# Half-chunks of two heads side by side in a triangular solve: 36 products per chunk in place of 72, and Q before K in one line

## The chip, the cores and the metric

One NeuronCore of one Trainium2 chip runs the whole program. The metric is the device time of one execution in microseconds; several executions are timed and their median is quoted.

## The reference

A delta-rule attention (4 batches, 8 heads, 768 tokens, head size 48) feeds two wide layers (384 to 2048 and back), one after the other.

```python
for t in range(S):
    y[:, :, t] = einsum('bhd,bhde->bhe', q[:, :, t], state)
    v_old = einsum('bhde,bhd->bhe', state, k_n[:, :, t])
    state = state + beta_t * einsum('bhd,bhe->bhde', k_n[:, :, t], v[:, :, t] - v_old)
x = y.transpose(0, 2, 1, 3).reshape(B * S, H * D)
h = x @ w_in;  x = softplus(h) @ w_out          # first layer
h = x @ w2_in; out = (h * cos(h)) @ w2_out      # second layer
```

`k_n` is `k` divided by its norm, per head and token.

## The kernel before

**Tiles.** The 768 tokens go in 24 chunks of C = 32. The 128 rows of a tile are the 4 batches times the 32 tokens of a chunk, and the 8 heads stand beside each other in the columns (8 x 48 = 384). A product for one head is a 128x128 stationary operand with four 32x32 (or 32-row) blocks on its diagonal, one per batch, against 48 moving columns. Every operand is kept as a pair of f16, a high and a low part, so a product is three passes, high by high, low by high and high by low (`HI_FIRST`): 3 x 8 = 24 PE products for all heads.

**Block diagonals.** The stationary tiles (`bdK`, `bdQ`, `bdA`, `bd2`, `bdG`, `bdT`) are zeroed once; then each chunk's rows are written into the diagonal blocks by DMAs in pieces of 64 f16. K and Q rows go from the buffer `kq` to DRAM (`kqd`) and back into `bdKQ`; keys, the masked scores and the coupling G go from `kp` through `kpd` into `bd2` and `bdG` (`load_2`); T goes through `tgd` into `bdT`, and for some odd chunks into a second tile that lies in `raw` (`bdU`).

**The solve.** Within a chunk, u has to solve a unit lower triangular 32x32 system per head and batch. It is cut into two halves of 16 tokens. `take_A` takes both diagonal 16x16 blocks of the Gram matrix (`abuf`) and the block that couples the halves (`kg`, later `bdG`). `solve` inverts the diagonal blocks for four chunks at once on VectorE, giving T. `step` then applies T to b, G to the result, adds that to b, and applies T again: the groups T, G, T, 24 products each, 72 in all. In all three the 16 upper tokens of a head and its 16 lower tokens share one 32x32 block. `take_b` and `take_u` split b and u into high and low parts between the groups: a ScalarE or VectorE copy for the high part, a VectorE subtraction for the low part.

**A chunk's serial path** (`step`, line 727): K rows by state into `psC0` (40 products), `bt` = that less v, `take_b`, T into `psC1`, `take_u`, G into `psC0`, `bt` plus that, `take_b`, T into `psC1`, `take_u`, the state update into `psC0` and `psC1` (48 products), the new state and its f16 parts, and on to the next chunk. The outputs y (Q rows by state, then scores by u) collect in `psY`. Two chunks fill a block of 256 tokens, which `moe_block(0, j)` sends through the first layer (`psH`, `accA`, `accB`). When all are done, the second layer runs six blocks of 512 tokens.

**Rows of a chunk.** `prep_k` transposes K on VectorE into `kq`: lines 554 to 557 write the main part and a tail of 8C columns. `prep_q` scales Q into the other row of the same buffer, and line 569 sends the first 32C columns of both rows to `kqd`. The buffer of chunk n is `kq[n % 4]`, [128, 2, 40C].

**Order.** Nothing is issued where it is written: `put` records operations with their keys, and a planner (`Plan`, lines 60 to 269) lists them per engine by estimated costs, with a priority from the backward pass. Where an operation may run on ScalarE or VectorE (`copy`), the planner also chooses the engine. The tile framework then adds the waits between the instructions that it finds to touch the same memory. Engines run their lists in order. All DMAs stand in SyncE's list.

Of the kernel before, what the change touches and what calls it, by code (L numbers as in the profile page):

```python
# [10 lines left out]
F32 = mybir.dt.float32  # L11
# [9 lines left out]
P = 128  # L21
# [267 lines left out]
def delta_moe_moe_kernel(ctx, tc, q, k, v, beta, mask, ident, w1, w2, out):  # L289
# [15 lines left out]
    mask_sb = const.tile([P, C + 4], F32, name="mask_sb")  # L305
# [19 lines left out]
    bdK, bdQ = bdKQ[:, 0], bdKQ[:, 1]  # L325
    bdA2 = att.tile([P, 44, B, X2], F16, name="bdA2")
# [8 lines left out]
    bt = att.tile([P, H, D], F32, name="bt")  # L335
    b16 = att.tile([P, 2, H, D], F16, name="b16")
# [6 lines left out]
    kpf = [pre.tile([P, 64 * C], F16, name=f"kp{i}") for i in range(4)]  # L343
    kpb = [x[:, 0:48 * C].rearrange("p (s h d l) -> p s h d l", s=3, h=H, l=2) for x in kpf]
    kgb = [x[:, 48 * C:].rearrange("p (h t l) -> p h t l", h=H, l=2) for x in kpf]
    kab = [pre.tile([P, H // 2, C, 2], F16, name=f"ka{i}") for i in range(2)]
    kqb = [pre.tile([P, 2, Z], F16, name=f"kq{i}") for i in range(4)]
# [27 lines left out]
    kpd = dr.tile([NS, P, C * 64], F16, name="kpd")  # L375
# [183 lines left out]
    def prep_q(n):  # L559
# [4 lines left out]
        qv = kq[:, 1, 0:32 * C].rearrange("p (s h t l) -> p s h t l", s=2, t=C, l=2)  # L564
# [3 lines left out]
        if n >= 4:  # L568
            dma(kqd[n].rearrange("p (s z) -> p s z", s=2), kq[:, :, 0:32 * C], [("kqd", n)],
                [("kq", s, i) for i in range(3)] + [("pre",)], 1.46, issue=0.8, slack=1.5, **A)  # L570
        elif n:
            dma(kqd[n, :, 0:32 * C], k_main(n), [("kqd", n, 0)], k_keys(n)[:1], 0.73, **A)
            dma(kqd[n, :, 32 * C:], kq[:, 1, 0:32 * C], [("kqd", n, 1)], [("kq", s, 1), ("kq", s, 2), ("pre",)], 0.73, **A)
# [67 lines left out]

    def take_P(n, ps, pk):
# [3 lines left out]
        tt(pm, ps, mask_sb[:, 0:C].unsqueeze(1).to_broadcast([P, H, C]), ALU.mult, [("sq",)],  # L646
# [5 lines left out]
            + [("kp", s, i) for i in (*range(2, 6), "z")] + [("pre",)], 1.46, slack=1.5, **A)  # L652

    def solve(g):
# [3 lines left out]
        put([("DVE", 0.602)], [("m",)], [("abuf", i) for i in range(4)] + PR, lambda e: nc.vector.transpose(  # L658
# [68 lines left out]
    def step(n):  # L727
# [337 lines left out]
```

## Time and profile before

| | us |
|---|---|
| median of 3 runs | 1021.29 (1019.23 to 1028.05) |
| the profiled execution | 1025.06 |
| its span, first to last instruction | 1023.3 |
| TensorE (PE) busy | 957.5 |
| VectorE (DVE) busy | 661.5 |
| ScalarE (ACT) busy | 675.1 |
| GpSimd (POOL) busy | 348.6 |

Busy times are sums over one execution. A row of the timeline gives start, duration, engine, line, operation, output<-inputs, and in brackets the time that its engine sat idle before it and what ended that. PEld is PE's loading of stationary operands, which runs beside its products. SPq is SyncE's queue, which issues the DMAs. [...]

### The profile page before, as it was taken

How to read it: one execution, taken by the hardware profiler on the slowest of the kernel's cores; microseconds unless marked ns; L12 is line 12 of the kernel's file. 1: busy time of each engine (PE TensorE's matmuls, PEld its weight loads, DVE VectorE, ACT ScalarE, POOL GpSimd, SP SyncE). 2: the span in 40 equal slices, each digit the busy share in tenths (PEclk: the TensorE clock that was granted, in tenths of full speed). 3: DMA queues.
4: the chain of work that ended last, by engine and by line, in shares of the span. 5: the costliest groups of instructions: out<-in, count | busy, mean ns of one | idle time of the engine just before them, and what ended most of it. 6: DMA issues, size and time to landing. Idle time of an engine off the chain costs nothing.

```text
span 1023.3 us, 27706 instructions
## 1 busy us (share of the span) xinstructions
PE 957.5 (94%) x11624; PEld 690.2 (67%) x11624; DVE 661.5 (65%) x1193; ACT 675.1 (66%) x1278; POOL 348.6 (34%) x323
## 2 busy tenths in 40 slices
PE   1777987999999999999999999999999999999998
PEld 1446976989889898999998888644444444444443
DVE  8899974568548755964766665785555555455554
ACT  5375766677868877786768778866555555455554
POOL 4012135224423632362233334553332323323232
PEclk9788998999999999999999999999999999999999
DMA  6988896785777678577678942111001010000000
GB/s 201 304 242 201 172 255 137 166 213 123 179 163 163 134 179 180 110 149 158 134 179 209 211 99 78 47 62 62 1 10 53 1 62 1 32 31 1 31 1 31
DMA packets 317164, 121.91 MB, mean 119 GB/s; under 512 B 281456, under 2 KB 297072, under 8 KB 317040
## 3 DMA queue, kind: packets, MB, share of 16 engines
q1 hardware_dynamic: 317040, 120.15, 48.6%
q8 instruction: 91, 1.49, 0.6%
q14 instruction: 33, 0.27, 0.1%
HBM read 73.45 MB, written 37.22 MB: 108 GB/s over the span
## 4 chain that ended last, share of the span: by engine, by line
PE 59%; DVE 10%; ACT 8%; SPq 8%; DMA 8%; issue 4%; POOL 2%; DVEq 0%; ACTq 0%; POOLq 0%
PE psH L827 15%; PE accA L889 12%; PE accB L889 9%; SPq L384 7%; PE psC L827 7%; PE psA L889 6%; PE psC L710 4%; PE psY L827 4%; PE psY L710 2%; DMA qt<-q_dram 1%; DMA kt<-k_dram 1%; DMA w<-w_dram 1%; PE psA L622 1%; ACT e L416 1%; DVE g L405 1%
## 5 line engine op out<-in xcount | busy, mean ns | idle before, releaser
L405 POOL TENSOR_TENSOR g<-g,g 128x512 f16<-128x512 f32 x189 | 227.3, 1203 | 508.9 <-ACT g L393 507.6
L827 PE MATMUL psH<-xt,w 128*128 128x256 f16 x1728 | 224.3, 273 | 0.0
L393 ACT ACTIVATE g<-g 128x512 f16<-128x512 f32 x191 | 120.1, 629 | 115.6 <-DVE g L409 69.2
L889 PEld LDWEIGHTS <-w 128*128 128x128 f16 x1728 | 160.7, 98 | 21.7 <-issue 2.8
L827 PEld LDWEIGHTS <-w 128*128 128x128 f16 x1728 | 158.3, 97 | 17.6 <-issue 0.2
L889 PE MATMUL accA<-g,w 128*128 128x256 f16 x1152 | 156.3, 274 | 2.3 <-POOL g L405 2.3
L889 PEld LDWEIGHTS <-v 128*128 128x128 f16 x864 | 84.5, 98 | 102.4 <-issue 0.5
L827 PEld LDWEIGHTS <-v 128*128 128x128 f16 x864 | 84.5, 98 | 100.4
L414 ACT ACTIVATE e<-e 128x512 f32<-128x512 f32 x96 | 60.4, 629 | 82.0 <-DVE e L409 81.9
L405 DVE TENSOR_TENSOR g<-psH,e 128x512 f32<-128x512 f32 x96 | 66.1, 688 | 59.4 <-ACT e L416 50.4
L889 PE MATMUL accB<-g,w 128*128 128x256 f16 x576 | 93.3, 273 | 0.0
L710 PEld LDWEIGHTS <-bdA 128*128 128x128 f16 x2256 | 74.5, 98 | 17.9 <-issue 14.6
L827 PE MATMUL psH<-xu,v 128*128 128x512 f16 x351 | 83.4, 379 | 0.0
L827 PE MATMUL psC<-xu,v 128*128 128x512 f16 x342 | 82.1, 379 | 0.0
L889 PE MATMUL accA<-g,v 128*128 128x512 f16 x288 | 78.0, 379 | 0.3 <-POOL g L405 0.3
L889 PE MATMUL accB<-g,v 128*128 128x512 f16 x288 | 77.8, 379 | 0.0
L889 PE MATMUL psA<-g,v 128*128 128x512 f16 x288 | 77.7, 379 | 0.0
L844 ACT ACTIVATE e<-psH 128x512 f32<-128x512 f32 x96 | 56.5, 588 | 29.9 <-PE psH L827 29.7
L416 ACT ACTIVATE e<-e,hpi 128x512 f32<-128x512 f32 x96 | 69.1, 721 | 2.9
L710 PE MATMUL psC<-u,bdA 128*128 128x48 f16 x1680 | 59.9, 185 | 9.7 <-DMA bdA<-kpd 4.1
L710 PEld LDWEIGHTS <-bdKQ 128*128 128x128 f16 x1840 | 58.7, 97 | 5.6 <-issue 3.5
L416 ACT ACTIVATE e<-e 128x512 f32<-128x512 f32 x96 | 59.9, 624 | 1.2
(151 smaller groups left out, 1479.5 us busy)
## 6 DMA issues: line engine op xcount, KB each, us to landing
kpd<-kp SPq DMA_DIRECT2D x24, 512.0 KB, 4.6
bdA<-kpd SPq DMA_DIRECT2D x96, 128.0 KB, 4.1
bdKQ<-kqd SPq DMA_DIRECT2D x92, 128.0 KB, 4.0
kqd<-kq SPq DMA_DIRECT2D x20, 512.0 KB, 4.7
raw<-w_dram SPq DMA_DIRECT2D x12, 768.0 KB, 5.0
w<-w_dram SPq DMA_DIRECT2D x10, 768.0 KB, 7.1
v<-w_dram SPq DMA_DIRECT2D x10, 768.0 KB, 6.0
qt<-q_dram SPq DMA_DIRECT2D x24, 256.0 KB, 4.5
```

The source lines that it names most:

```text
L384: put([("SP", issue)], w, r, lambda e: nc.sync.dma_start(out=dst, in_=src), dma=eng_us, **kw)
L393: nc.scalar.activation(out=out, in_=in_, func=AF.Copy, scale=scale)
L405: put(var, w, r, lambda e: eng[e].tensor_tensor(out=out, in0=a, in1=b, op=op), port=True, **kw)
L414: nc.scalar.activation(out=out, in_=in_, func=func, scale=scale)
L416: nc.scalar.activation(out=out, in_=in_, func=func, scale=scale, bias=bias)
L622: nc.tensor.matmul(ps[:, h], lhsT=w, rhs=x, start=(i == 0), stop=(i == len(ops) - 1))
L710: nc.tensor.matmul(ps[:, h, 0:D], lhsT=lhs(h), rhs=mov[:, h], start=(first and i == 0 and h == 0), stop=(last and i == len(passes) - 1 and ...
L827: nc.tensor.matmul(hp[:, i] if ph == 0 else hp, lhsT=w[:, l, kc * P:(kc + 1) * P], rhs=xv[:, m * KC + kc], start=(kc == 0 and idx == 0), s ...
L844: nc.scalar.activation(out=ev, in_=hv, func=AF.Abs, scale=sc)
L889: nc.tensor.matmul(acc[c], lhsT=w[:, l, c * P:(c + 1) * P], rhs=rhs, start=(f == 0 and idx == 0 and (ph == 1 or c != 1)), stop=(f == NF - ...
```

## The change

Two heads, h and h + 4, now share a 32-row block in the solve. The host stores the tokens so that in heads 4 to 7 the two halves of each chunk are exchanged for K (`turned`), and for v and beta the second half of the rows also exchanges the heads (`crossed`). Columns 0 to 3 (half 0) then hold the first halves of all eight heads, columns 4 to 7 the second halves. T, G and T work on four columns each: T on half 0, G from its result, T on half 1, 12 products apiece, 36 per chunk.

What has to cross between a head and its partner is done by VectorE with a column of `mask_sb` as scalar that is zero in one half of the rows (`sel`). `bt` takes two instructions per half, `un` gathers u in the original places (two copies and two sums), and `take_A` takes its blocks in halves of four heads. `kpd` shrinks from 64C to 56C columns, `bdG` from 8 to 4 blocks, and the memsets of the unused half of `kg` go.

The buffer `kq` becomes one row of 72C columns: Q in 0 to 32C, K in 32C to 64C, the tail of K in 64C to 72C, so the transfer to `kqd` is one piece per row. Where the order was K, Q it is now Q, K.

```diff
-Z = 40 * C
+Z = 72 * C
-    kpf = [pre.tile([P, 64 * C], F16, name=f"kp{i}") for i in range(4)]
+    kpf = [pre.tile([P, 56 * C], F16, name=f"kp{i}") for i in range(4)]
-    kqb = [pre.tile([P, 2, Z], F16, name=f"kq{i}") for i in range(4)]
+    kqb = [pre.tile([P, Z], F16, name=f"kq{i}") for i in range(4)]
...
-            dma(kqd[n].rearrange("p (s z) -> p s z", s=2), kq[:, :, 0:32 * C], [("kqd", n)],
+            dma(kqd[n], kq[:, 0:64 * C], [("kqd", n)],
...
-        return kqb[n % 4][:, 0] if n >= 4 else kg0[n // 2][:, n % 2]
+        return kqb[n % 4][:, 32 * C:] if n >= 4 else kg0[n // 2][:, n % 2]
...
+    def sel(i):
+        return mask_sb[:, M0 + i:M0 + i + 1]
...
     def take_A(n, ps, pk):
-        copy(av, ps[:, :, 0:N2], mask_sb[:, C + 1:C + 2], [("abuf", i)], r, 128, ps=True, **A)
-        stt(av, ps[:, :, N2:], mask_sb[:, C + 2:C + 3], av, ALU.mult, ALU.add, [("abuf", i)], r, 128, **A)
-        kg, first_rows = kg[:, :, N2:], mask_sb[:, C + 3:C + 4]
-        copy(kg[:, :, :, 1], ps[:, :, N2:], first_rows, [("kp", s, 4)], r, 128, ps=True, **A)
-        stt(kg[:, :, :, 0], ps[:, :, N2:], first_rows, kg[:, :, :, 1], ALU.mult, ALU.subtract, [("kp", s, 5)],
-            r + [("kp", s, 4)], 128, **A)
+        copy(av, ps[:, :, 0:N2], sel(1), [("abuf", i, 0), ("abuf", i, 1)], r, 128, ps=True, **A)
+        for a in range(2):
+            to, fro = slice(HH * a, HH * a + HH), slice(HH * (1 - a), HH * (1 - a) + HH)
+            stt(av[:, to], ps[:, fro, N2:], sel(2), av[:, to], ALU.mult, ALU.add, [("abuf", i, a)], r, 64, **A)
+        for a in range(2):
+            x = ps[:, HH * a:HH * a + HH, N2 * (1 - a):N2 * (2 - a)]
+            kc = kg[:, :, N2 * (1 - a):N2 * (2 - a)]
+            copy(kc[:, :, :, 1], x, sel(3 + a), [("kp", s, 4 + a)], r, 64, ps=True, **A)
+            stt(kc[:, :, :, 0], x, sel(3 + a), kc[:, :, :, 1], ALU.mult, ALU.subtract, [("kp", s, 6 + a)],
+                r + [("kp", s, 4 + a)], 64, **A)
...
-    def group(ps, key, passes, first=True, last=True):
+    def group(ps, key, passes, first=True, last=True, heads=H):
...
     def step(n):
-            stt(bt, r[:, :, 0:D], 1.0 / (K_SC * S_SC), vt, ALU.mult, ALU.subtract, [("bt",)],
-                [("psC", 0)] + vk, DM, **A)
...
+        for a in range(2):
+            x, y = bt[:, half[a]], vt[:, half[a]]
...
+                stt(x, r[:, half[1 - a], 0:D], sel(6), y, ALU.mult, ALU.subtract, [("bt", a)],
+                    [("psC", 0), ("mask",)] + vk, DM // 2, **A)
+                stt(x, r[:, half[a], 0:D], sel(5), x, ALU.mult, ALU.add, [("bt", a)], [("psC", 0), ("mask",)], DM // 2, **A)
+            if a == 0:
+                take_b(0)
...
-        group(u, ("psC", 1), by_T)
-        take_u()
-        x = ps_c[0]
-        group(x, ("psC", 0), [(lambda h, l=l: col(bdG, h, l), u16[:, m], bk("bdG") + [("u16", m)])
-                              for l, m in HI_FIRST])
-        stt(bt, x[:, :, 0:D], 1.0 / (K_SC * S_SC), bt, ALU.mult, ALU.add, [("bt",)], [("psC", 0)], DM, **A)
-        take_b()
-        group(u, ("psC", 1), by_T)
+        group(u, ("psC", 1), by_T(0), heads=HH)
+        uf = u[:, 0:HH, 0:D]
+        copy(uf16[:, 0], uf, 1.0 / T_SC, [("uf", 0)], uk, DM // 2, ps=True, **A)
+        stt(uf16[:, 1], uf, 1.0 / T_SC, uf16[:, 0], ALU.mult, ALU.subtract, [("uf", 1)], uk + [("uf", 0)], DM // 2, **A)
+        for a in range(2):
+            copy(un_[:, half[a]], uf, sel(7 + a), [("un", a)], uk + [("mask",)], DM // 2, ps=True, **A)
+        group(r, ("psC", 0), [(lambda h, l=l: col(bdG, h, l), uf16[:, m], bk("bdG") + [("uf", m)])
+                              for l, m in HI_FIRST], heads=HH)
+        x = bt[:, half[1]]
+        stt(x, r[:, 0:HH, 0:D], 1.0 / (K_SC * S_SC), x, ALU.mult, ALU.add, [("bt", 1)], [("psC", 0)], DM // 2, **A)
+        take_b(1)
+        group(r, ("psC", 0), by_T(1), heads=HH)
...
-        take_u()
+        for a in range(2):
+            x = un_[:, half[a]]
+            stt(x, r[:, 0:HH, 0:D], sel(8 - a), x, ALU.mult, ALU.add, [("un", a)], [("psC", 0), ("mask",)], DM // 2, **A)
+        UN = [("un", a) for a in range(2)]
+        copy(u16[:, 0], un_, 1.0, [("u16", 0)], UN, DM, **A)
+        tt(u16[:, 1], un_, u16[:, 0], ALU.subtract, [("u16", 1)], UN + [("u16", 0)], DM, only=("DVE",), **A)
```

**How the order moves.** VectorE, chunk 8, where K is transposed into its buffer (`kq_127` before, `kq_129` after: kp is the main part, ka the tail). The brackets name the semaphores that a row waits for; DMAHW stands for a transfer. Before:

```order
295 L409 SCALAR_TENSOR_TENSOR u_110<-psC_144,u_110 128x384 [waits Activation_49]
296 L555 STREAM_TRANSPOSE kq_127<-kp_121 128x512 [waits Pool_49]
297 L409 SCALAR_TENSOR_TENSOR bt<-psC_143,bt 128x384 [waits PE_49]
298 L557 STREAM_TRANSPOSE kq_127<-ka_125 128x128 [waits DMAHW6_49,Activation_49]
299 L409 SCALAR_TENSOR_TENSOR b_109<-bt,b_109 128x384 [waits Activation_49]
300 L405 TENSOR_TENSOR g_93<-psH_138,e_95 128x512 [waits Activation_49]
```

And after:

```order
338 L409 TENSOR_TENSOR u_112<-un,u_112 128x384 [waits Activation_49]
339 L561 STREAM_TRANSPOSE kq_129<-ka_127 128x128 [waits Activation_49]
340 L559 STREAM_TRANSPOSE kq_129<-kp_123 128x512 [waits Pool_49]
341 L413 SCALAR_TENSOR_TENSOR st<-psC_145,st 128x384 [waits PE_49]
342 L413 SCALAR_TENSOR_TENSOR st<-psC_146,st 128x384 [waits PE_49]
343 L413 SCALAR_TENSOR_TENSOR st_105<-st_105,mask_sb,st 128x384 [waits Activation_49]
```

The tail's transpose (row 298, now 339) no longer waits for a transfer; before it stood between `bt` and the low part of b, now behind the chunk's last u. SyncE, the transfer of chunk 8's rows to `kqd` and what stands around it, before:

```order
97 L384 DMA qt_116<-q_dram 128x512
98 L384 DMA kqd<-kq_130 256x1x1024
99 L384 DMA x2d<-xs 768x1x256
100 L384 DMA kqd<-kq_127 256x1x1024
101 L384 DMA bdA_102<-kq_127 32x12x64 x4
102 L384 DMA bdT<-tgd 32x8x64 x4
```

And after:

```order
106 L388 DMA bdA_102<-kpd 32x28x64 x4
107 L830 DMA_TRANSPOSE xt_92<-y_113 128x6x128
108 L388 DMA bdA_102<-kq_129 32x12x64 x3
109 L388 DMA vt_107<-v_dram 128x384
110 L388 DMA kqd<-kq_129 128x2048
```

The transfer now goes in 128 pieces of 2048 elements in place of 256 of 1024, and stands behind the loads of `bdA` from the same buffer (three of four are in this piece) instead of ahead of them. VectorE again, chunk 17, from `bt` (K rows by state less v) to the last u, with instructions of the first layer (g) between them, before:

```order
694 L409 SCALAR_TENSOR_TENSOR bt<-psC_143,vt_107 128x384
695 L409 SCALAR_TENSOR_TENSOR b_109<-bt,b_109 128x384
696 L409 SCALAR_TENSOR_TENSOR u_110<-psC_144,u_110 128x384
697 L405 TENSOR_TENSOR g_93<-psH_138,e_95 128x512
698 L409 SCALAR_TENSOR_TENSOR bt<-psC_143,bt 128x384
699 L409 SCALAR_TENSOR_TENSOR b_109<-bt,b_109 128x384
700 L409 SCALAR_TENSOR_TENSOR u_110<-psC_144,u_110 128x384
```

And after, in two pieces: up to the low part of b of half 0, and from the low part of uf on.

```order
776 L413 SCALAR_TENSOR_TENSOR bt<-psC_145,mask_sb,vt_107 128x192
777 L413 SCALAR_TENSOR_TENSOR bt<-psC_145,mask_sb,bt 128x192
778 L413 SCALAR_TENSOR_TENSOR bt<-psC_145,mask_sb,vt_107 128x192
779 L561 STREAM_TRANSPOSE kq_131<-ka_127 128x128
780 L413 SCALAR_TENSOR_TENSOR bt<-psC_145,mask_sb,bt 128x192
781 L413 SCALAR_TENSOR_TENSOR b_111<-bt,b_111 128x192
```

```order
785 L413 SCALAR_TENSOR_TENSOR uf_110<-psC_146,uf_110 128x192
786 L559 STREAM_TRANSPOSE kq_132<-kp_126 128x512
787 L413 SCALAR_TENSOR_TENSOR bt<-psC_145,bt 128x192
788 L413 SCALAR_TENSOR_TENSOR b_111<-bt,b_111 128x192
789 L413 SCALAR_TENSOR_TENSOR un<-psC_145,mask_sb,un 128x192 x2
790 L409 TENSOR_TENSOR g_94<-psH_141,e_96 128x512
791 L409 TENSOR_TENSOR u_112<-un,u_112 128x384
```

Six instructions of the step have become eleven, most of half the size; both sums for half 1 and a transpose of K now stand ahead of b's low part.

## Rows read from the trace of the kernel before

**Rows 1.** The page: span, busy time of each engine, and forty slices in tenths

```profile
span 1023.3 us, 27706 instructions
...
PE 957.5 (94%) x11624; PEld 690.2 (67%) x11624; DVE 661.5 (65%) x1193; ACT 675.1 (66%) x1278; POOL 348.6 (34%) x323
...
PE   1777987999999999999999999999999999999998
```

**Rows 2.** Busy time by stage (window, length, busy us and count by engine, clock, DMA)

```profile
0.00:100.00 100.00, 57.92 (x936) 40.65 (x937) 92.32 (x192) 54.50 (x121) 20.27 (x24) 0.88 0.86 240
100.00:300.00 200.00, 183.91 (x3230) 166.51 (x3227) 134.07 (x275) 144.96 (x304) 70.30 (x73) 0.97 0.78 176
300.00:650.00 350.00, 346.24 (x5746) 314.65 (x5744) 227.14 (x424) 268.60 (x536) 133.73 (x125) 1.00 0.67 150
650.00:1023.00 373.00, 369.45 (x1724) 168.43 (x1722) 207.92 (x303) 207.03 (x320) 124.32 (x103) 1.00 0.08 27
```

**Rows 3.** The same by stage for instructions on b alone: PE, DVE, ACT

```profile
0.00:100.00 100.00, 4.19 (x96) 4.00 (x7) 1.54 (x3) 0.88 0.86 240
100.00:300.00 200.00, 15.20 (x408) 10.92 (x16) 8.27 (x16) 0.97 0.78 176
```

**Rows 4.** Who PE waited for from 100 to 300 us: total, times, longest

```profile
PE psC L710 <- DVE b L409: 6.3, 1, 6.3
```

**Rows 5.** Timeline of PE around 461 us

```profile
461.44 0.56 PE L710 MATMUL psC<-u,bdA 128*128 128x48 f16 x16
461.84 0.36 PE L710 MATMUL psY<-st,bdKQ 128*128 128x48 f16 x8
```

**Rows 6.** Timeline around 161 us, then DVE's waits for transfers of 100 to 300

```profile
161.95 1.00 SPq L384 DMA_DIRECT2D kqd<-kq  x1
...
167.13 0.31 DVE L557 STREAM_TRANSPOSE kq<-ka 128x128 f32<-128x128 f32 x1 [8.22 <-DMA kqd<-kq]
...
167.94 0.48 PE L710 MATMUL psC<-b,bdT 128*128 128x48 f16 x8 [6.26 <-DVE b L409]
...
DVE kq L557 <- DMA kqd<-kq: 8.2, 1, 8.2
```

**Rows 7.** Busy time by stage around that place

```profile
160.00:168.00 8.00, 1.74 (x30) 1.45 (x29) 0.87 (x3) 1.98 (x6) 1.93 (x3) 0.90 0.72 238
168.00:174.00 6.00, 6.00 (x96) 5.00 (x96) 2.50 (x6) 4.22 (x10) 2.69 (x3) 0.56 0.36 55
```

**Rows 8.** Groups by shape: output<-inputs, shapes, count | busy us, mean ns | idle before

```profile
L409 DVE SCALAR_TENSOR_TENSOR b<-bt,b 128x384 f16<-128x384 f32 x48 | 34.8, 724 | 21.8 <-ACT b L393 21.6
L409 DVE SCALAR_TENSOR_TENSOR u<-psC,u 128x384 f16<-128x384 f32 x48 | 26.5, 552 | 30.2 <-ACT u L393 30.0
L393 ACT ACTIVATE b<-bt 128x384 f16<-128x384 f32 x46 | 23.7, 514 | 10.3 <-DVE bt L409 9.8
L393 ACT ACTIVATE u<-psC 128x384 f16<-128x384 f32 x48 | 23.1, 482 | 9.5 <-PE psC L710 9.4
L409 DVE SCALAR_TENSOR_TENSOR bt<-psC,vt 128x384 f32<-128x384 f32 x23 | 12.6, 548 | 5.4 <-PE psC L710 5.3
L409 DVE SCALAR_TENSOR_TENSOR abuf<-psA,mask_sb,abuf 128x128 f32<-128x128 f32 x21 | 9.4, 448 | 3.2 <-ACT abuf L393 3.2
L393 ACT ACTIVATE kp<-psA,mask_sb 128x128 f16<-128x128 f32 x21 | 8.5, 403 | 4.3 <-DVE abuf L409 3.7
L409 DVE SCALAR_TENSOR_TENSOR kp<-psA,mask_sb,kp 128x128 f16<-128x128 f32 x21 | 7.3, 349 | 1.4 <-ACT kp L393 1.4
```

**Rows 9.** Timeline of chunk 17: the last u and the state update

```profile
466.21 0.56 DVE L409 SCALAR_TENSOR_TENSOR u<-psC,u 128x384 f16<-128x384 f32 x1 [1.97 <-ACT u L393]
...
473.78 0.77 PE L710 MATMUL psC<-u,bdA 128*128 128x48 f16 x24
```

**Rows 10.** The page: all packets, and the DMA issues that read kpd

```profile
DMA packets 317164, 121.91 MB, mean 119 GB/s; under 512 B 281456, under 2 KB 297072, under 8 KB 317040
...
bdA<-kpd SPq DMA_DIRECT2D x96, 128.0 KB, 4.1
```

More of the change, by code (lines that the diff above doesn't have):

```diff
@@ L374, in delta_moe_moe_kernel @@
     kqd = dr.tile([NS, P, 64 * C], F16, name="kqd")
-    kpd = dr.tile([NS, P, C * 64], F16, name="kpd")
+    kpd = dr.tile([NS, P, C * 56], F16, name="kpd")
     tgd = dr.tile([NG, P, 4, C * 16], F16, name="tgd")
@@ L651, in take_P @@
         dma(kpd[n], kpf[s], [("kpd", n)], [("kp", s, l, t) for l in range(2) for t in range(2)]
-            + [("kp", s, i) for i in (*range(2, 6), "z")] + [("pre",)], 1.46, slack=1.5, **A)
+            + [("kp", s, i) for i in range(2, 8)] + [("pre",)], 1.28, slack=1.5, **A)
     def solve(g):
@@ L657, in solve @@
         PR = [("pre",)]
-        put([("DVE", 0.602)], [("m",)], [("abuf", i) for i in range(4)] + PR, lambda e: nc.vector.transpose(
+        put([("DVE", 0.602)], [("m",)], [("abuf", i, a) for i in range(4) for a in range(2)] + PR, lambda e: nc.vector.transpose(
             out=m.rearrange("p j i -> p (j i)"), in_=abuf.rearrange("p j m -> p (j m)")), **A)
@@ L712, in fn @@
                         start=(first and i == 0 and h == 0),
-                        stop=(last and i == len(passes) - 1 and h == H - 1))
-            put([("PE", 8 * mm(D))], [key], r, fn, cold=1.55, **A)
+                        stop=(last and i == len(passes) - 1 and h == heads - 1))
+            put([("PE", heads * mm(D))], [key], r, fn, cold=1.55, **A)
     def load_2(n):
-        bd_load(bdA2[:, 12:], ("bd2", "bdG"), kpd[n], [("kpd", n)], 0.9, issue=0.75)
+        bd_load(bdA2[:, 12:], ("bd2", "bdG"), kpd[n], [("kpd", n)], 0.8, issue=0.72)
     def by_state(bd, key):
@@ L787, in step @@
                 else:
-                    stt(st16[:, 1, c], st16[:, 0, c], mask_sb[:, C:C + 1], st[:, c], ALU.mult, ALU.add,
+                    stt(st16[:, 1, c], st16[:, 0, c], sel(0), st[:, c], ALU.mult, ALU.add,
                         [("st16", 1, c)], [("st", c), ("st16", 0, c), ("mask",)], DM, **A)
@@ L956, in delta_moe_moe_kernel @@
     load_v(1)
-    first = ((bdK, "bdK"), (bdQ, "bdQ"), (bdA, "bdA"), (bdA22[:, 1], "bd2"))
+    first = ((bdQ, "bdQ"), (bdK, "bdK"), (bdA, "bdA"), (bdA22[:, 1], "bd2"))
     norms(0)
@@ L970, in delta_moe_moe_kernel @@
     for n in range(4):
-        ps, pk = gram(n, first[n][0], first[n][1], (0,))
+        ps, pk = gram(n, first[n][0], first[n][1], (1,))
         take_A(n, ps[:, :, 0], pk)
@@ L975, in delta_moe_moe_kernel @@
         prep_q(n)
-        ps, pk = gram(n, first[n][0], first[n][1], (1,))
+        ps, pk = gram(n, first[n][0], first[n][1], (0,))
         take_P(n, ps[:, :, 0], pk)
@@ L985, in prep @@
         ps, pk = gram(n, bdA, "bdA", (0, 1))
-        take_A(n, ps[:, :, 0], pk)
-        take_P(n, ps[:, :, 1], pk)
+        take_A(n, ps[:, :, 1], pk)
+        take_P(n, ps[:, :, 0], pk)
     def open_wp2(e):
@@ L1022, with turned, crossed @@
     from concourse.bass_utils import run_bass_kernel_spmd
+    def turned(a):
+        a = np.array(a).reshape(B, H, NS, C, -1)
+        a[:, H // 2:] = np.roll(a[:, H // 2:], C // 2, axis=3)
+        return a
+    def crossed(a):
+        a = turned(a)
+        a[:, :, :, C // 2:] = np.roll(a[:, :, :, C // 2:], H // 2, axis=1)
+        return a
     def tok(a):
-        a = np.asarray(a).transpose(2, 0, 1, 3).reshape(NS, C, B, H, D)
-        return np.ascontiguousarray(a.transpose(0, 2, 1, 3, 4)).reshape(NS, P, DM)
+        return np.ascontiguousarray(a.transpose(2, 0, 3, 1, 4)).reshape(NS, P, DM)
     def q_rows(a):
@@ L1038, in w_both @@
         return np.ascontiguousarray(np.stack([wi, wo], axis=2))
-    be = np.asarray(inputs["beta"]).reshape(B, H, NG, 4, C).transpose(0, 3, 1, 2, 4)
+    be = crossed(inputs["beta"]).reshape(B, H, NG, 4, C).transpose(0, 3, 1, 2, 4)
+    later = np.triu(np.full((C, C), 1.0 / K_SC, np.float32), 1)
+    sc = K_SC ** -2, 1.0 / K_SC, 1.0 / (K_SC * S_SC), 1.0 / T_SC
+    which = np.zeros((2, 9), np.float32)
+    which[1, 0] = -1.0
+    for i, x in enumerate(sc):
+        which[0, 1 + 2 * i] = which[1, 2 + 2 * i] = x
     arrays = {
         "q_dram": q_rows(inputs["q"]),
-        "k_dram": tok(inputs["k"]),
-        "v_dram": tok(inputs["v"]),
+        "k_dram": tok(turned(inputs["k"])),
+        "v_dram": tok(crossed(inputs["v"])),
         "beta_dram": np.ascontiguousarray(be).reshape(P, NG, C),
-        "mask_dram": np.tile(np.concatenate([
-            np.triu(np.full((C, C), 1.0 / K_SC, np.float32), 1),
-            np.repeat(np.array([[0.0, K_SC ** -2, 0.0, 1.0 / K_SC], [-1.0, 0.0, K_SC ** -2, 0.0]], np.float32), C // 2, axis=0)],
-            axis=1), (B, 1)),
+        "mask_dram": np.tile(np.concatenate([later, np.roll(later, C // 2, axis=0), np.repeat(which, C // 2, axis=0)],
+                                            axis=1), (B, 1)),
         "ident_dram": W_SC * np.eye(P, dtype=np.float32),
```

61 lines of the change are left out of this document (32 added, 29 removed).

## The prediction, made before the run

> **What bounds the kernel now.** I began with the page: of a span of 1023.3 us TensorE (PE) is busy 957.5, and in its row of forty slices, 25.6 us each, it falls short of full in the first seven alone, and a little in the last [rows 1]. So the whole is PE-bound, except at the start. The second view, busy time by stage, says how much: PE stands idle 42.1 us of the first 100, 16.1 us from 100 to 300, 3.8 us from 300 to 650, and 3.6 us after that [rows 2]. From 650 us the second layer runs alone; the change touches nothing there, and those 373 us stay. In the first 100 us VectorE (DVE) is busy 92.3 us and the DMA engines 86%, so there PE waits for them.
>
> The change works on the products of the triangular solve. Taking the products that read b by stage shows 96 of them before 100 us and 408 from 100 to 300 [rows 3]. A chunk has 48 such products, 24 chunks have 1152, so 648 are left for the third stage: 2 chunks fall into the first stage, 8.5 into the second, 13.5 into the third.
>
> Third, the waits of PE from 100 to 300 us: one of 6.3 us for VectorE's b is the largest by far [rows 4]. I looked at that place in the timeline, because an in-order engine that stands still for so long is either starved or blocked; it is told below.
>
> **The products.** Per chunk T, G and T were 72 products of 128x48 and become 36. Their price is not the busy time of a group (0.56 us for sixteen), which holds the pipe's depth once, but the distance between starts: sixteen start at 461.44 and the next group at 461.84, thus 25 ns each [rows 5]. 36 x 25 ns = 0.90 us a chunk: 1.8, 7.7 and 12.2 us in the three stages, 21.7 us in all. What is left to gain depends on how far PE sets the pace there. In the first stage I count nothing, since PE waits anyway. In the second PE is busy 183.9 of 200 us, 0.92, which makes 7.1; in the third 346.2 of 350, 0.99, which makes 12.0. Together 19.1 us, between 12.0 (the third stage alone) and 21.7.
>
> **The chain inside a chunk.** This holds only if the serial path of a chunk does not get longer, since half as many products are now fed by more, smaller vector instructions. Path before, from bt to the second u high, by rows: bt 0.548, b high 0.514, b low 0.724 (beside 16 products), the last 8 products 0.20, u high 0.482, u low 0.552, 0.20, bt again 0.548, 0.514, 0.724, 0.20, 0.482 [rows 8]: 5.69 us. The trace has no 192-column form. On VectorE 128 columns take 349 ns and 384 take 548, so 192 lie near 0.40 (estimate, on the line between them); the other 128-column row, 448, is the upper end. In the same way b low goes from 0.72 to 0.57, and ScalarE's copies, 403 ns at 128 and 482 to 514 at 384, to 0.42 to 0.45. After: two bt 0.80, 0.45, 0.57, 0.10, 0.42, 0.40, 0.10, 0.40, 0.45, 0.57, 0.10, two un 0.80, u high 0.51: 5.67 us. No difference. There is also room: in chunk 17 u is ready at 466.77, and the first product of the state update starts at 473.78 [rows 9]. For 7 us PE had other work which the order puts first.
>
> **What VectorE and ScalarE get.** The built order has 163 more instructions on VectorE (1,195 to 1,358) and 68 more on ScalarE. Per chunk on VectorE: the step had 3.65 us in six instructions (2 x 0.548 + 2 x 0.724 + 2 x 0.552) [rows 8] and gets about 5.06: four for bt, one for G's sum, uf low and two un at 0.40 each, two b low at 0.57, and u low at 0.72 as b low's row has it. take_A had 0.448 + 0.349 and gets four of 64 columns near 0.35: +0.6. So +2.0 us a chunk, 48 us in all. From 100 us on VectorE has that room (134 of 200 busy, then 227 of 350), and PE hides it. In the first 100 us it has not: four take_A and two steps are 2.4 + 2.8 = 5.2 us on an engine with 7.7 us idle. I take +3, between -1 (the memsets that go, the PE gain) and +6.
>
> [...]
>
> **The blocked VectorE.** At 158.9 us VectorE stops for 8.2 us in front of a transpose into kq, which waits for the transfer kqd<-kq issued at 161.95. Behind it stands b low, for which PE waits 6.26 us [rows 6]. The transposed piece is the tail of K, columns 32C to 40C of the buffer's first row; the transfer reads columns 0 to 32C of both rows, so the tail lies between what it reads and is not part of it. Yet the transpose waits. With Q and K in one line the transfer reads 0 to 64C and the tail lies behind it. The order bears that out: the same transpose of chunk 8 loses its DMA wait (the first pair of order pieces above; the second pair shows the transfer itself, which also stands later now). [...] The place is worth up to 6.26 + 2.6 = 8.9 us, and nothing if another wait stands right behind. I take two thirds, 6, because the order behind it is made anew and the other 9.8 us that PE idles from 100 to 300 us (16.1 less 6.3) come from waits of the same kinds.
>
> **Transfers.** kpd shrinks by an eighth (64C to 56C). Its reads are 96 x 128 KB, its writes as much, so 3 of 121.9 MB go. A piece of bdA lands 4.1 us after its issue [rows 10], beside PE work; zero, and at best 2 us in the first stage where DMA is 86% busy. The new issue order of all queues is the planner's; I give it no sign, but 4 us either way.
>
> **Sum.** -19.1 (products) - 6 (blocked VectorE) + 3 (start) = -22.1 us. On the profiled execution, 1025.06 us with its span of 1023.3, that is 1003; its median over three runs is 1021.29, 3.8 lower, so I forecast 1021.3 - 22.1 = 999 us.
>
> **The rivals.**
> - Another wait takes the place of the blocked one. For it: the transposes wait for other transfers too, and the start has been reshuffled. Against: it is the one VectorE wait on kqd from 100 to 300 us, and one single wait [rows 6]. Then -19.1 + 3: 1005 us.
> - The stages before 300 us stay bound by VectorE and DMA and gain nothing, and the start loses 6. For it: 92.3 and 86% there; against: 0.92 on PE after it. -12.0 + 6: 1015 us.
> - All goes well: 21.7 + 8.9 and no loss at the start: 991 us.
> - Slower: the chain of a chunk becomes the bound. Three more vector instructions stand on it than before (12 for 9), and each can queue behind another one of 0.72 us [rows 8]: 2.2 us; at the upper end of 0.45 the eight small ones add 0.4. It decides only from about 3.5 us a chunk, half of the 7 us of rows 9, if every second chunk has such room and the others none. That takes one or two queueings more in every chunk. At 4.5 us it would cost 1 us in each of 22 chunks in place of the gain: 1021 + 22 = 1043.
> That the products do not go is no rival: the order lists 21,450 PE instructions in place of 23,178, which is 2 x 36 x 24 fewer.
>
> **Chances.** Forecast 0.50, another wait 0.20, the early stages bound 0.16, all well 0.09, slower 0.05. Range 988 to 1014: low end the best case with 2 to 3 us from transfers, high end the second rival. About 1% (10 us) is what a measurement tells from no change. Faster by more holds in the forecast, in the first rival, the best case and a little of the second: 0.80; within 1%: 0.15; slower 0.05.
>
> **What would show it.** In the new profile: about 10,760 PE products; PE busy near 935; VectorE up by some 45 us; the stage from the start to the second layer's takeover shorter by about 22 us, and its remaining 373 us unchanged; no VectorE wait on kqd; the 0.56 clock after 168 us gone. I would be wrong if PE waits beyond 300 us grew past 10 us, above all waits for u or b (then the chain bounds), or if the first layer's first products (psH) came more than 6 us later than now (then the start does).

## The result, and the profile after

| | before | after |
|---|---|---|
| median, us | 1021.95 (1019.18 to 1028.05) | 1004.71 (1002.24 to 1008.98) |
| profiled execution, us | 1025.06 | 1004.13 |
| its span, us | 1023.3 | 1001.9 |

The ratio is 0.9834, 95% interval 0.9801 to 0.9867: 17.2 us faster by the medians, where 22.1 were forecast. Sign and range held; the point lies 5.7 us too low. The profiled execution of before was 3.1 us above its median, that of after 0.6 below, so the two traces differ by more, 21.4 us of span, than the kernels do.

The page of the changed kernel, to be held against [rows 1]:

```profile
span 1001.9 us, 26170 instructions
...
PE 934.9 (93%) x10760; PEld 666.7 (67%) x10760; DVE 679.5 (68%) x1356; ACT 682.0 (68%) x1346; POOL 354.2 (35%) x326
```

The products are the 10,760 of the forecast, and PE is busy 22.6 us less. VectorE rose by 18 us, not by the 48 forecast. The same by stage, against [rows 2]; the last stage, the second layer alone, is taken to begin 21 us earlier:

```profile
0.00:100.00 100.00, 54.68 (x852) 37.13 (x853) 92.41 (x212) 55.17 (x126) 20.21 (x22) 0.86 0.87 247
100.00:300.00 200.00, 189.99 (x3198) 171.55 (x3195) 151.94 (x353) 158.88 (x356) 77.64 (x79) 0.99 0.76 175
300.00:629.00 329.00, 321.83 (x4999) 290.41 (x5000) 228.43 (x491) 261.44 (x548) 132.93 (x123) 1.00 0.63 149
629.00:1001.00 372.00, 368.36 (x1715) 167.57 (x1713) 206.75 (x303) 206.52 (x319) 123.43 (x103) 1.00 0.08 27
```

From 100 to 300 us PE is busier than before (190.0 against 183.9 of 200), although it has fewer products: waits went. From 300 us on it is the other way round: 7.2 us idle in 329, where before had 3.8 in 350. The waits of PE of after, first from 100 to 300 us, then from 300 to 650, against [rows 4]:

```profile
PE psC L724 <- ACT u L397: 2.6, 2, 1.9
PE psH L855 <- DVE g L409: 2.3, 2, 1.2
PE psC L724 <- ACT st L397: 1.5, 1, 1.5
...
PE psC L724 <- DMA bdKQ<-kqd: 3.4, 2, 2.1
PE psC L724 <- DMA bdA<-kpd: 2.5, 2, 2.3
```

The 6.3 us for VectorE's b are gone, and VectorE no longer waits for kqd. What PE waits for late are two transfers.

For where the time went I use a landmark that both kernels have: the transpose of `abuf` with which each group of four chunks begins (line 658 before, 672 after). Its rows in the timelines of before and of after:

```profile
L658 DVE STREAM_TRANSPOSE mlan<-abuf x6: 711/712/714, 30.1 to 500.5; 128x512 f32<-128x512 f32 x6
```

```profile
L672 DVE STREAM_TRANSPOSE mlan<-abuf x6: 694/711/712, 29.3 to 484.8; 128x512 f32<-128x512 f32 x6
```

The last two numbers of time are the first and the last start. The six starts give the table below, in us, for these two and for six of the experiments that follow. A gap is four chunks; "rest" goes from the last landmark to the end of the span.

| kernel | first | gap 1 | gap 2 | gap 3 | gap 4 | gap 5 | rest |
|---|---|---|---|---|---|---|---|
| before | 30.1 | 90.3 | 102.9 | 94.0 | 92.3 | 90.8 | 522.8 |
| after | 29.3 | 93.0 | 94.7 | 89.8 | 89.3 | 88.8 | 517.1 |
| layout alone | 30.1 | 91.6 | 97.5 | 92.5 | 93.7 | 90.9 | 521.0 |
| products cut | 30.6 | 94.3 | 101.1 | 91.8 | 91.2 | 89.5 | 522.4 |
| solve alone | 30.7 | 94.1 | 93.8 | 92.3 | 89.1 | 92.2 | 520.7 |
| idle products | 28.9 | 93.8 | 92.6 | 92.8 | 91.9 | 90.9 | 519.4 |
| kpd old size | 29.8 | 96.2 | 93.7 | 91.7 | 90.0 | 88.8 | 519.3 |
| longer chain | 29.6 | 96.8 | 96.3 | 91.9 | 90.1 | 89.3 | 518.9 |

Of the 21.4 us, 0.8 lie ahead of the first landmark; 8.2 come from gap 2, in which the blocked VectorE lay; 9.2 from gaps 3 to 5, where PE is busiest; 5.7 from the rest; gap 1 gave 2.7 back. Each line is one execution, and a profiled one can lie some us off its median (solve alone: 1015.1 against 1006.4), so single gaps are read to 2 or 3 us, and the verdicts below go by the ratios.

### The profile page after: what moved, and what is told of

The parts are those of the page before. It is cut to its first block, busy times and chain, and to the rows that moved or that the text cites. A ratio compares the mean times of both kernels' runs of the same rounds, so it can differ in the third digit from the quotient of the medians.

```text
span 1001.9 us, 26170 instructions
## 1 busy us (share of the span) xinstructions
PE 934.9 (93%) x10760; PEld 666.7 (67%) x10760; DVE 679.5 (68%) x1356; ACT 682.0 (68%) x1346; POOL 354.2 (35%) x326
## 5 line engine op out<-in xcount | busy, mean ns | idle before, releaser
L855 PE MATMUL psH<-xt,w 128*128 128x256 f16 x1728 | 219.9, 272 | 4.3 <-DVE g L409 2.4
L917 PEld LDWEIGHTS <-w 128*128 128x128 f16 x1728 | 163.1, 98 | 21.4 <-issue 2.0
L724 PEld LDWEIGHTS <-bdA 128*128 128x128 f16 x1968 | 63.2, 98 | 19.1 <-issue 17.1
L413 DVE SCALAR_TENSOR_TENSOR g<-psH,e 128x512 f32<-128x512 f32 x39 | 27.0, 691 | 49.6 <-ACT e L420 49.6
```

The lines of the kernel that those rows point to most:

```text
L413: lambda e: nc.vector.scalar_tensor_tensor(out, in0=a, scalar=s, in1=b, op0=op0, op1=op1), port=True, **kw)
L724: nc.tensor.matmul(ps[:, h, 0:D], lhsT=lhs(h), rhs=mov[:, h], start=(first and i == 0 and h == 0), stop=(last and i == len(passes) - 1 and ...
L855: nc.tensor.matmul(hp[:, i] if ph == 0 else hp, lhsT=w[:, l, kc * P:(kc + 1) * P], rhs=xv[:, m * KC + kc], start=(kc == 0 and idx == 0), s ...
L917: nc.tensor.matmul(acc[c], lhsT=w[:, l, c * P:(c + 1) * P], rhs=rhs, start=(f == 0 and idx == 0 and (ph == 1 or c != 1)), stop=(f == NF - ...
```

## The experiments

Each ratio is to the kernel before, run beside it on the same chip (one chip for e1 to e4, a second for e5 to e8, a third for f1 to f4). Where two ratios are compared, the half width is the root of the two half widths' squares summed, and 0.001 is 1.02 us.

**e1, layout alone.** The kernel before with K and Q in one line; the order on VectorE, ScalarE and GpSimd is untouched.

```diff
-    bdK, bdQ = bdKQ[:, 0], bdKQ[:, 1]
+    bdQ, bdK = bdKQ[:, 0], bdKQ[:, 1]
-    kqb = [pre.tile([P, 2, Z], F16, name=f"kq{i}") for i in range(4)]
+    kqb = [pre.tile([P, Z], F16, name=f"kq{i}") for i in range(4)]
```

> The kernel before (72 products, old solve) with the one-line buffer alone: Q, K and K's tail in one row; the order of VectorE, ScalarE and GpSimd is that of before, row for row. Theory (the products set the pace, and the blocked VectorE is a second, smaller gain): VectorE's 8.2 us wait for kqd is gone and the time falls by 2 to 9 us, 1013 to 1020. Rival 1 (nearly all of the gain is that blocked wait): about 1006. Rival 2 (the gain comes from the new order of the queues): no change, 1022.

1020.23 us, ratio 0.9962 (0.9938 to 0.9987): 3.9 us. VectorE's wait for kqd is gone (not one is left in the trace), and gap 2 is 5.4 us shorter. The fall lies within the theory's 2 to 9 us; the first rival falls, and the second, no change, lies just outside the interval. The edit also halves the number of pieces of the transfer, but a sooner landing is not what ended the wait:

```profile
159.04 1.11 SPq L384 DMA_DIRECT2D kqd<-kq  x1
159.32 0.31 DVE L557 STREAM_TRANSPOSE kq<-ka 128x128 f32<-128x128 f32 x1 [0.33 <-ACT ka L393]
...
160.96 0.98 SPq L384 DMA_DIRECT2D kqd<-kq  x1
```

The tail's transpose starts 0.3 us after one of the two transfers is issued and before the other, and no transfer of kqd in this trace lands in less than 2.6 us (4.3 in the median). With the order of these engines the same, this shows that the wait came from the tail of K lying between the two pieces that the transfer reads.

**e2, products cut.** The kernel before in its own order, with 36 products per chunk fewer.

```diff
-                for h in range(H):
+                for h in ((0, H - 1) if cut and i else range(H)):
```

> The kernel before with 36 of the 72 products left out: in the groups T, G, T the two passes with a low part run for heads 0 and 7 alone, so u lacks most of its low parts. Costs given to the planner, and so the order of all engines, are those of before; the vector instructions and the two-row buffer stay. Theory: 0.90 us a chunk, 12 to 21.7 us less, likeliest 19: 1003 (1000 to 1010). Rival 1 (blocked wait): 1022, at most 4 less. Rival 2 (new order): 1022, at most 4 less.

1020.47 us, ratio 0.9954 (0.9931 to 0.9976): 4.7 us, where the products were held to be worth 19. The page of this kernel, then a wait of VectorE and the first three of PE (100 to 300 us):

```profile
PE 939.8 (92%) x10760; PEld 668.2 (65%) x10760; DVE 661.7 (65%) x1193; ACT 673.1 (66%) x1278; POOL 348.4 (34%) x323
```

```profile
DVE kq L557 <- DMA kqd<-kq: 6.6, 1, 6.6
...
PE psC L710 <- DVE b L409: 5.6, 1, 5.6
PE psC L710 <- ACT u L393: 3.6, 2, 3.0
PE psC L710 <- ACT b L393: 2.1, 3, 0.9
```

PE works 17.7 us less than before, and the span is 2.4 us shorter: the freed time turned into waits. PE is idle 4.5 us more than before in the first 100 us, 4.6 more from 100 to 300 (there for b and u above all), and 6.3 more from 300 to 629, where the waits are spread over transfers, g and u.

**e3, solve alone.** The changed kernel with the old buffer of two rows, in the order of after.

```diff
-    kqb = [pre.tile([P, Z], F16, name=f"kq{i}") for i in range(4)]
+    kqb = [pre.tile([P, 2, Z], F16, name=f"kq{i}") for i in range(4)]
```

> The changed kernel with the old two-row buffer for K and Q; VectorE's, ScalarE's and GpSimd's order is that of the changed kernel. Theory: the products' gain stays, a wait of K's tail for kqd can come back: 1005 plus 0 to 9, likeliest 1008. Rival 1: 1018 or more. Rival 2 (order): 1005.

1006.4 us, ratio 0.9829 (0.9792 to 0.9866), the same as the whole change. VectorE waits for kqd nowhere here either, although the tail lies between the pieces again: in this order the transposes into kq of that stretch stand from 166 to 177 us and wait for no transfer. So the layout is worth 4 us in the old order and nothing that shows (-0.5 +- 5 us) on top of the new solve.

**e4, idle products.** The changed kernel in its own order, with 12 products more ahead of each of T, G and T, whose results are overwritten: 72 per chunk again.

```diff
+                if heads == HH and i == 0:
+                    for x in range(12):
+                        nc.tensor.matmul(ps[:, x % HH, 0:D], lhsT=lhs(x % HH), rhs=mov[:, x % HH],
+                                         start=(x == 0), stop=(x == 11))
```

> The changed kernel with 12 idle products of 128x48 in front of each of the groups T, G, T, so 72 a chunk again; the result is overwritten by the group's own first product, and the order of all engines stays that of the changed kernel. Theory: 36 x 25 ns x 24 = 21.7 us come back where PE sets the pace: 1005 + 15 to 22, 1020 to 1027. Rivals 1 and 2: at most 1010.

1012.72 us, ratio 0.9882 (0.9849 to 0.9914). Against after (0.9834) the products are worth 0.0048 +- 0.0047, some 5 us; and with all 72 of them the new form is still 12 us faster than before. The stages of this kernel:

```profile
100.00:300.00 200.00, 194.07 (x3514) 178.16 (x3515) 150.20 (x353) 158.08 (x351) 75.69 (x78) 1.00 0.74 175
300.00:500.00 200.00, 196.50 (x3551) 181.06 (x3549) 141.35 (x343) 156.46 (x350) 79.41 (x82) 1.00 0.67 143
```

In the table its gaps 3 to 5 are 7.7 us longer than after's (0.64 us a chunk), its gaps 1 and 2 are 1.3 us shorter. So far as one trace tells, the products count late and not early. The time lies between the theory's range and the rivals'. The idle products need the high part alone, so PE can run them while the low part is still being made. In after's trace it does so with a group's own products: one b low runs from 265.88 to 267.10 us, the first eight products of its T start at 266.63 and the last four, which read it, at 267.77. For the idle products themselves this is not shown; what a product costs elsewhere in a group was not measured.

**e5 and e6, the same two with the planner told.** The costs in `put` follow the products that are there, and the order is made anew. The edit of e5:

```diff
-            put([("PE", 8 * mm(D))], [key], r, fn, cold=1.55, **A)
+            put([("PE", (2 if cut and i else 8) * mm(D))], [key], r, fn, cold=1.55, **A)
```

> As e2 (36 of the 72 products left out, the two low passes of T, G, T run for heads 0 and 7 alone, old vector instructions and buffer), but the planner is given the smaller cost (2 products for such a pass in place of 8), so all queues are listed anew for it. Revised theory (the products are the gain, but only an order made for them turns freed PE time into a shorter time): 1003 to 1010 on a before of 1022 to 1025, 12 us or more below e2. Rival L (any new order moves the time by this much, by luck): anywhere from 1010 to 1030, no nearer to the changed kernel than the two kernels with another boost. Rival R (the new form of the solve, its halves and its buffers, is what shortens the time): about e2, 1017 to 1021.

> As e4 (the changed kernel with 12 idle products in front of each of T, G, T), but the planner is given their cost and lists all queues anew. Revised theory: it becomes no faster than e4, and with luck equal to it, 1012 to 1026. Rival L: as likely below 1010 as above. Rival R: 1005 to 1012.

e5 took 1024.43 us, ratio 1.0007 (0.9989 to 1.0025); e6 1017.94, 0.9932 (0.9907 to 0.9956). Each lost some 5 us to its twin by a new order alone. That the old form needed only a fitting order to profit from the cut, the revised theory, is not borne out by e5. But e6 lies in that theory's range, and rival R, the new form itself, missed both of its own (1017 to 1021 and 1005 to 1012). With the order made for them, the same 36 products are worth nothing in the old form (e5 against before) and 0.0098 +- 0.0041, 10 us, in the new one (e6 against after). In e5 VectorE waits for kqd three times, 12.5 us together; this is the wait of [rows 6] in another order:

```profile
DVE kq L557 <- DMA kqd<-kq: 12.5, 3, 6.7
```

**e7, e8, f3, f4, other orders.** Both kernels with the planner's priority number changed.

```diff
-BOOST = 0.95
+BOOST = 0.96
```

> The kernel before with nothing but the planner's weight for attention work changed, BOOST 0.96 in place of 0.95: the same instructions in another order on every engine. Revised theory and rival R: within 5 us of before. Rival L: 8 us or more away from before, either way.

> The changed kernel with BOOST 0.96 in place of 0.95: the same instructions in another order. Revised theory and rival R: within 5 us of the changed kernel's 1005. Rival L: 8 us or more away, either way.

> The kernel before with the planner's one priority number at 0.94 in place of 0.95: a third order of the same instructions. Theories S and T: the orders spread little, ratio 0.997 to 1.006. Theory O: at least one order of the old form comes near the new form's, 0.985 to 0.992.

> The changed kernel with the planner's one priority number at 0.94: a third order of the new form. Theories S and T: within 4 us of the changed kernel, ratio 0.979 to 0.987. Theory O: it may lose the gain, 0.990 to 1.000.

| | 0.94 | 0.95 | 0.96 |
|---|---|---|---|
| before | 1.0043 (1.0024 to 1.0063) | 1 | 1.0036 (1.0017 to 1.0055) |
| after | 0.9819 (0.9792 to 0.9846) | 0.9834 (0.9801 to 0.9867) | 0.9806 (0.9784 to 0.9828) |

Three orders of one form lie within 0.5%, the two forms at the same number 1.7 to 2.3% apart. All four lie where the revised theory, S and T had them. So rivals L and O fall: the gain belongs to the new form and is not the luck of one order. Its size does depend on the order: at 0.94 and 0.96 it is 23 us in place of 17.

**f1, kpd at its old size.** The changed kernel in its own order; kp, kpd and the tile behind bdA have their old sizes, and an eighth of what is moved is read by no product. Four small memsets at the start fill that part.

```diff
-    kpf = [pre.tile([P, 56 * C], F16, name=f"kp{i}") for i in range(4)]
+    kpf = [pre.tile([P, 64 * C], F16, name=f"kp{i}") for i in range(4)]
-    kpd = dr.tile([NS, P, C * 56], F16, name="kpd")
+    kpd = dr.tile([NS, P, C * 64], F16, name="kpd")
```

> The changed kernel with its order untouched on every engine, and only the kpd transfers back at their old size (128 KB in place of 112 KB in each direction, with a part that no product reads). Theory S (the rest of the gain, about 10 us beside the products, is the shorter chain of one chunk: 5.2 us measured against 5.69): no difference, ratio 0.982 to 0.986. Theory T (the rest of the gain is the smaller transfers, since the tensor engine's last waits between 300 and 650 us are for bdA from kpd and bdKQ from kqd): about 10 us of the gain goes, ratio 0.990 to 0.995. Theory O (only the order of the plan): no difference, 0.982 to 0.986.

1016.76 us, ratio 0.9916 (0.9889 to 0.9943): 0.0082 +- 0.0043 of the gain goes, 8.4 us, about half of it. That is what theory T expected, and neither S nor O. Against f4, the new form's other order on this same chip, it is 0.0097 +- 0.0038. The page and the transfers of after, then of f1, and f1's waits of PE for that transfer (first 100 us, 100 to 300, 300 to 629):

```profile
DMA packets 302310, 118.68 MB, mean 118 GB/s; under 512 B 269168, under 2 KB 284784, under 8 KB 302192
...
bdA<-kpd SPq DMA_DIRECT2D x96, 112.0 KB, 3.5
```

```profile
DMA packets 314598, 121.83 MB, mean 121 GB/s; under 512 B 281456, under 2 KB 297072, under 8 KB 314480
...
bdA<-kpd SPq DMA_DIRECT2D x96, 128.0 KB, 3.6
```

```profile
PE psC L724 <- DMA bdA<-kpd: 5.6, 1, 5.6
...
PE psC L724 <- DMA bdA<-kpd: 2.4, 1, 2.4
...
PE psC L724 <- DMA bdA<-kpd: 3.0, 1, 3.0
```

One transfer takes hardly longer (3.6 against 3.5 us), but there are 3.15 MB more to move, in 12,288 more packets, all of them under 512 B; at the 175 GB/s of after's second stage that is 18 us of moving (an estimate). Whether it is the bytes or the packets that cost, f1 does not tell. PE waits 11.0 us in all for bdA from kpd, after 6.2 (3.7 of them in the first 100 us): 4.8 of the 7.7 us by which the spans differ. In the table the loss is spread: 3.2 us in gap 1, 1.9 in gap 3.

A rival stands for part of it, the clock. Over the whole execution the granted TensorE clock (1.00 is full speed) is 0.976 to 0.978 in five of f1's six runs and 0.983 in the sixth; in after's six it is 0.983 to 0.988. In the traces the difference lies at the start. The first 100 us of f1 and of f2, the next experiment, to be held against the 0.86 of after:

```profile
0.00:100.00 100.00, 55.86 (x830) 37.36 (x831) 90.83 (x213) 55.01 (x124) 20.75 (x22) 0.81 0.83 245
```

```profile
0.00:100.00 100.00, 55.62 (x771) 36.33 (x772) 91.02 (x210) 55.91 (x128) 19.80 (x22) 0.81 0.84 237
```

f2 moves the small transfers, has the same 0.81, and its gap 1 is even longer than f1's. So it is not shown that the 3.2 us of gap 1 are the price of the transfers, nor whether the larger transfers are what lowers the clock.

**f2, a longer chain.** The changed kernel in its own order; three copies on a chunk's path are made twice, first into a spare tile.

```diff
+            if twice and e == "ACT":
+                nc.scalar.activation(out=spare[e], in_=in_, func=AF.Copy, scale=scale)
```

> The changed kernel with its order untouched, but each of three copies on the chain of a chunk (the first part of b for either half, the first part of uf) is made twice, first into a spare tile: 3 x 0.32 to 0.36 us, about 1.0 us more chain per chunk, 24 us in all, with 24 us more work on the scalar engine. Theory S: the chain is what paces, so the time grows by 12 to 24 us, ratio 0.995 to 1.007. Theories T and O: the chain has slack, and the time grows by less than 5 us, ratio 0.982 to 0.988.

1011.54 us, ratio 0.9858 (0.9829 to 0.9887): 0.0024 +- 0.0044 over after, 2.5 us. Theory S wanted at least 12. Added were, by the groups of this kernel, 24 us on ScalarE:

```profile
L398 ACT ACTIVATE spareACT<-bt 128x192 f16<-128x192 f32 x46 | 16.7, 363 | 9.5 <-DVE bt L418 9.1
...
L398 ACT ACTIVATE spareACT<-psC 128x192 f16<-128x192 f32 x23 | 7.4, 322 | 0.4 <-PE psC L729 0.4
```

That is 1.0 us a chunk by the rows, and 0.7 by ScalarE's busy time on the page (698.7 against 682.0 us), since rows overlap. So a chunk's path takes up most of a microsecond more at little cost, and the half microsecond by which it became shorter explains little of the gain.

## Why the prediction was right, and where not

**What bounds.** Right as a reading, wrong as a price. PE was the busiest engine everywhere from 100 us on; but "In the second PE is busy 183.9 of 200 us, 0.92, which makes 7.1; in the third 346.2 of 350, 0.99, which makes 12.0" took the busy share for the share of freed time that reaches the end. This is the step that failed. The 19.1 us measured 4.7 in the old form (e2) and 4.9 (0.1 to 9.6) in the new (e4 against after), and 10 (5.8 to 14.2) in the new with the order made anew (e6 against after). Late, a chunk gained 0.64 us by e4 and 0.38 by e2 (gaps 3 to 5, 277.1 to 272.5), not 0.89; early it gained nothing that the traces tell. The share says that PE is ahead of the others; it does not say how closely they follow.

**The price of a product.** 25 ns was somewhat high: e2 has 864 fewer and PE's busy time falls by 17.7 us, e4 864 more and it grows by 18.3, thus 21 ns each.

**The chain: "No difference."** Its length was over-estimated and its slack rightly seen. The groups of after, against [rows 8]:

```profile
L413 DVE SCALAR_TENSOR_TENSOR b<-bt,b 128x192 f16<-128x192 f32 x48 | 24.0, 500 | 10.9 <-ACT b L397 10.8
L413 DVE SCALAR_TENSOR_TENSOR bt<-psC,mask_sb,bt 128x192 f32<-128x192 f32 x46 | 19.0, 412 | 1.0
L413 DVE SCALAR_TENSOR_TENSOR bt<-psC,mask_sb,vt 128x192 f32<-128x192 f32 x46 | 18.7, 407 | 7.9 <-PE psC L724 7.5 <-issue 0.2
...
L413 DVE SCALAR_TENSOR_TENSOR un<-psC,mask_sb,un 128x192 f32<-128x192 f32 x48 | 17.8, 410 | 5.8 <-PE psC L724 5.6
L397 ACT ACTIVATE b<-bt 128x192 f16<-128x192 f32 x46 | 16.7, 363 | 8.9 <-DVE bt L413 8.4
L409 DVE TENSOR_TENSOR u<-un,u 128x384 f16<-128x384 f32 x24 | 14.9, 621 | 4.7 <-ACT u L397 4.4
...
L413 DVE SCALAR_TENSOR_TENSOR abuf<-psA,mask_sb,abuf 128x64 f32<-128x64 f32 x42 | 12.2, 328 | 13.0 <-ACT abuf L397 13.0
L413 DVE SCALAR_TENSOR_TENSOR kp<-psA,mask_sb,kp 128x64 f16<-128x64 f32 x42 | 12.0, 286 | 7.5 <-ACT kp L397 7.2
L397 ACT ACTIVATE u<-un 128x384 f16<-128x384 f32 x22 | 11.5, 524 | 7.3 <-DVE un L413 7.3
...
L413 DVE SCALAR_TENSOR_TENSOR uf<-psC,uf 128x192 f16<-128x192 f32 x24 | 8.5, 354 | 9.9 <-ACT uf L397 9.8
L413 DVE SCALAR_TENSOR_TENSOR bt<-psC,bt 128x192 f32<-128x192 f32 x24 | 8.4, 350 | 7.2 <-PE psC L724 6.9
L397 ACT ACTIVATE uf<-psC 128x192 f16<-128x192 f32 x23 | 7.4, 322 | 0.4 <-PE psC L724 0.4
```

b low takes 0.500 in the mean (0.57 estimated), the sums without a column of the mask 0.35 (0.40), ScalarE's copies 0.32 to 0.36 (0.42 to 0.45), the sums with such a column 0.41 as forecast. In the forecast's own order of steps that is 5.2 us a chunk against 5.69. f2 shows that such a half microsecond decides little, so the rival in which the chain becomes the bound was rightly held small.

The mean of b low, like the 0.724 of [rows 8] from which it was estimated, is not the price of the instruction. By minimum, median and maximum, and at one place of the timeline:

```profile
L413 DVE SCALAR_TENSOR_TENSOR b<-bt,b x48: 309/358/1668, 25.4 to 574.1; 128x192 f16<-128x192 f32 x48
...
L413 DVE SCALAR_TENSOR_TENSOR uf<-psC,uf x24: 336/357/359, 57.7 to 571.9; 128x192 f16<-128x192 f32 x24
```

```profile
265.72 1.16 POOL L409 TENSOR_TENSOR g<-g,g 128x512 f16<-128x512 f32 x1 [2.94 <-ACT g L397]
265.88 1.22 DVE L413 SCALAR_TENSOR_TENSOR b<-bt,b 128x192 f16<-128x192 f32 x1 [0.52 <-ACT b L397]
```

Half of them take 0.36 us or less, like uf low. In after's trace 15 of the 48 take 0.45 to 1.67 us, and each of these runs beside an instruction of GpSimd, as here; in before it is 17 of 48, over a median of 0.559. No instruction of the step that reads psC is drawn out in this way: on VectorE none of 192 columns takes more than 0.42 us in after. So a chunk's chain is longer where GpSimd's work meets a b low.

**VectorE.** "+2.0 us a chunk, 48 us in all" became 18. The step's seven kinds sum to 111 us in these rows, 24 more than 24 times 3.65, and take_A's two to 24.2 against 16.7 [rows 8]: 31 us, since the short forms are cheaper than estimated. Most of the other 13 is a matter of counting: all rows of VectorE together grow by 29 us, from 705 to 734, while the page counts the time in which two of them overlap only once. At 192 columns the trace has 350 and 354 ns in two rows and a median of 358 for b low, but 407 to 412 with a column of the mask. The start, "+3", is within what one trace tells: the first landmark 0.8 us earlier, gap 1 2.7 longer, and the first layer's first products at 99.6 us in place of 97.1.

**The blocked VectorE: -6.** Its cause is shown by e1, its size was 3.9 (1.3 to 6.4). But it does not show on top of the rest: e3 has the gain without it. The wait is a trap in the layout, into which an order falls or not (8.2 us in before, 12.5 in e5, 9.0 in e7, none in e3 and f3). Nor is an order without it a fast one: f3, the old form at 0.94, has no such wait and is no faster than e7. The clock after it did as forecast, though another dip stands earlier in after:

```profile
142.00:148.00 6.00, 5.50 (x79) 4.21 (x76) 4.99 (x8) 4.12 (x8) 4.56 (x5) 0.72 0.97 321
168.00:174.00 6.00, 6.00 (x103) 5.45 (x102) 5.42 (x13) 6.00 (x18) 5.20 (x7) 1.00 1.03 132
```

From 168 us on the clock is full, where [rows 7] had 0.56. That 0.56 is a mean over six us: in before the granted clock is 0.50 from 168 to 173 us and 0.88 in the sixth. The 2.6 us in the forecast's 8.9 are an estimate from it, 6.0 x (1 - 0.56), which no run shows by itself; what e1 shows is the 3.9 us for the whole place. In after the clock is 0.72 from 142 to 148, behind six us in which PE was busy 3.46.

**Transfers: "zero".** The second step that failed. The eighth of kpd was worth 8.4 us (4.0 to 12.7, f1). The forecast looked at one transfer's latency beside PE work; what f1 puts back are 3 MB in 12,288 packets on engines that are busy 63 to 87% until the second layer starts. How they reach the end of the kernel is shown in part only: PE's own waits for that transfer account for 4.8 us of the trace, and the clock at the start may have a share.

**The sum.** By the runs: products 5, transfers 8, together 13 of 17.2 us; the remaining 4 us lie within the errors of both, and no run assigns them (a new solve with full-width vector instructions, for one, was not tried). With e6 in place of e4 the products would be 10 and nothing would remain; two orders of one form differ by up to 5 us, so the runs do not decide between the two. The forecast had 19 and 0, with 6 for a wait that any new order might have removed, and +3: errors of opposite sign in a total that came out near, by luck. None of its signs of being wrong came (PE idles 7.2 us from 300 to 629 us, the first layer's first products are 2.5 us later), so they did not test the step that failed. The rival of 1005 had the number but not the reason. That of 1015 was right that the products gain nothing early, but its 12 us late measured 4.6 (e2) and 7.7 (e4) in gaps 3 to 5, and its loss of 6 at the start came out as 1.9 (first landmark and gap 1).

## What to carry to other kernels

A busy share of 0.99 says which engine leads, not how closely the next follows (12.0 us were forecast for that stage, and gaps 3 to 5 measured 4.6 and 7.7); before it is turned into a gain, take the work out alone in the old order, as e2 does, and see what the span does. Price a smaller transfer by what all its bytes and packets take from the engines that move them, not by the latency of one piece beside other work (f1: 8.4 us in all, at 3.6 us in place of 3.5 for one transfer). A planner's new order moved the time here by up to 5 us by itself, so parts of that size are judged over several orders, or with the order held. Look at median and maximum before a mean is taken for the price of an instruction (b low in after: 0.358 and 1.668 us, at a mean of 0.500).

## What the runs showed that was not expected

- 1/8 off one buffer's traffic (3.15 of 121.83 MB, 12,288 of 314,598 packets) went with a kernel 0.8% faster, with PE busy 93% of its span (f1 against after).
- 864 products more or fewer moved the time by only 5 us in an order kept as it was, although they moved PE's busy time by 18 (e2, e4).
- The subtraction that reads bt and b takes 0.36 us, and up to 1.67 us beside an instruction of GpSimd; the one that reads psC and uf never takes more than 0.36 (128x192 each, after).
